# A new word table for batches 2 to 5: the products with w of tiles 3 and 4 beside the next batch's products with v, tile 5 beside its second scores

## The chip, the cores and the metric

The kernel runs on one core of a Trainium2 chip. The metric is device time in microseconds (us), the median of several runs.

## The reference

Eight batches of attention in two stages, and a layer with a maximum of three products behind it. `sm_attn` is softmax attention with a row maximum; heads have 64 columns.

```python
p_packed = sm_attn(p, k, v)                 # 32 packed queries, 576 keys, 8 heads, 8 batches
out = sm_attn(q, p_packed, p_packed)        # 576 queries on the 32 packed rows
x = out.transpose(0, 2, 1, 3).reshape(B * S, H * D)          # 4608 x 512
h = maximum(maximum(x @ w1, x @ w2), x @ w3)                 # 4608 x 768
return h @ w_out                                             # 4608 x 512
```

## The kernel before

Per batch the work falls into stages, each a Python generator that issues some instructions and yields. A **word** of a table advances one generator by one step: a letter, the batch (0 this one, 1 the next) and what else it needs, and at its end `v`, `g` or `a` for VectorE (DVE), GpSimd (POOL) or ScalarE (ACT) where the engine can be chosen. `P03` is a step of this batch's `project` of tile 3, `V101` one of the next batch's `values`. The order of words is the order of instructions on every engine and DMA queue; `START` holds the words of batches 0 and 1 and `LOOP` those of one batch, run for b = 2 to 7. There is no other scheduler.

The stages that matter here, with their lines:

- `S` scores (L253), products of the packed queries with k; `A` weigh (L266 maximum, L271 exp); `X` spread (L315): DVE transposes the weights into `x`, which goes to DRAM as `xk` (L318) and comes back as `xt` in four transfers (L322).
- `V` values (L342): 80 products with v, 64 of form 128\*32 (rows by columns of the array) and then 16 of form 64\*32. `K` packed (L357): one transpose and a copy, `pt`.
- `Q` queries (L370): second scores, 32 products of form 64\*32. `B` attend: transposes into `e` (L393), maximum (L397), subtraction (L399, POOL unless told otherwise), exp, sum `z2` (L404), reciprocal, product (L413), transpose `et` (L416), and the operands `a2h` (L131 or L133) and `a2l` (L136).
- `P` project (L442): w is multiplied by the packed rows, 16 products of form 64\*32 for a tile; ACT makes `ph` (L453) and DVE `pl` (L455). Two halves (r = 0 and 1) of a tile go to two PSUM tiles of the pool `ps_moe` (four buffers) for tiles 0 and 3, to one of `ps_big` (two buffers) for the others.
- `N` layer_in (L477): the large products. Six tiles of 128 hidden columns, each six steps (half `hf`, matrix `i`) of six products of 128\*128 into one `ps_moe` buffer `mi{b}_{tile}_{hf}_{i}`. `E` maximum: a copy out of the first buffer (L131 on ACT, L133 on DVE) and two maxima (L491, DVE), into `r{b}_{pair of tiles}`.
- `H` halves (L515 differences, then `yah`, `yal`, ... by L131/L133 and L136); `O` layer_out (L546), 14 groups of 9 products; `F` finish, with the stores.

A "burst" below is a run of small products (forms other than 128\*128) between large ones. A product in `N` waits until the step that had its `ps_moe` buffer four buffers earlier has been copied or taken into a maximum.

Of the kernel before, what the change touches and what calls it, by code (L numbers as in the profile page):

```python
# [20 lines left out]
B, H, S, D, NP = 8, 8, 576, 64, 32  # L21
# [52 lines left out]


LOOP = """
S1 A10 N02 N02 N02 N02 A11 N02 E020v A10 E020 E020 N00 N00 E021v E000 Z10 X1 E021 N02 A11 P03 X1 P05 E021 H02v
P03 P04 N01 N00 v11 N00 v10 P03 P03 P03 E001 q10 N03 N03 N00 N00 H02g E000 N03 N03 N03 E030v E030 E010 N01 Z11
N03 E000 E001 E001 H00v H00 H02v E031v P04 q11 E030 H00 N01 E031 E031 P04 E010 E010 N01 N01 N01 E011 E011 E011
X1 V101 V101 H03g H03 N04 N04 N04 N04 P05 k20 K1 E041 N04 H03v N04 H01g H01v H01v K1 Q1 E040v H01 H01 H03 H03  # L80
P05 E040 E041 E040 E041 B11 B11 N05 N05 N05 N05 B10 E050 E050 H04 B10 E050 N05 B11 H04 H04 E051 E051 N05 E051
P10 B11 B10 P11 P12 H05 H05 B11 H05v P10 O0 O0 P10 O0 B10 B10 B11v H05v P12 P11 F0 B10v P10 O0 F0 H01v H03v
H05 O0 O0 F0 H05 B11 F0 P12 B10 k21 B10g O0 O0 O0 F0 P11 F0 F0 O0 B10 F0 B11g B11 F0 F0 B10g B10v P10 B11g F0
F0 O0 O0 O0 F0 F0 B11v O0 F0 F0
"""


# [1 line left out]
def fused_kernel(ctx: ExitStack, tc: tile.TileContext, kp, qt, va, vb, wi, wo, out):  # L89
# [48 lines left out]
    def doze(n):  # L138

        for i in range(0, n, 4):  # L140
            k = min(n - i, 4)
            ps = ps_moe.tile([P, 512], F32, name=f"idle{len(dozes)}", tag="moe")
            dozes.append(ps)
            nc.tensor.matmul(  # L144
                out=ps[:, 0:k * P], lhsT=ident, rhs=ident.unsqueeze(1).to_broadcast([P, k, P]),
                start=True, stop=True,
            )
# [280 lines left out]
    def project(b, j):  # L428

        parts = [slice(0, R)]  # L430
        if j == 0 and b != 1 or j == 3 and b >= 2:

            parts = [slice(r, r + 1) for r in range(R)]
            ps = [ps_moe.tile([P, 512], F32, name=f"pw{b}_{j}_{r}", tag="moe") for r in range(R)]
            src = [x[:, 0:NW * P].unsqueeze(1) for x in ps]
        else:
            x = ps_big.tile([P, R, 512], F32, name=f"pw{b}_{j}", tag="big")
            ps, src = [x[:, r] for r in range(R)], [x[:, :, 0:NW * P]]
        for n in range(4):
            for r in range(R):  # L440
                o = slice(64 * r, 64 * r + 64)
                nc.tensor.matmul(  # L442
                    out=ps[r][NP * n:NP * n + NP, 0:NW * P],
                    lhsT=pt_sb[b % 2][o, NP * n:NP * n + NP],
                    rhs=w_sb[o, j, n * NW * P:(n + 1) * NW * P],
                    start=True, stop=True,
                )
        yield 1
        hi = pool.tile([P, R, NW * P], F32R, name=f"ph{b}_{j}", tag="ph", bufs=3)
        lo = pool.tile([P, R, NW * P], F32R, name=f"pl{b}_{j}", tag="pl", bufs=3)  # L450
        pw[b, j] = (hi, lo)
        for r, x in zip(parts, src):
            nc.scalar.activation(out=hi[:, r], in_=x, func=AF.Copy, scale=2.0 ** -WS)  # L453
            yield 1
            nc.vector.scalar_tensor_tensor(  # L455
                out=lo[:, r], in0=x, scalar=2.0 ** -WS, in1=hi[:, r].bitcast(F32), op0=ALU.mult, op1=ALU.subtract,
            )
            yield 1
# [148 lines left out]
    def weigh_and_turn(b, r):  # L607
# [5 lines left out]
    stages = {  # L613
        "S": scores, "A": weigh_and_turn, "Z": invert, "X": spread, "V": lambda b, *rs: values(b, rs), "K": packed, "Q": queries,
        "B": attend, "C": convert, "P": project, "N": layer_in, "E": maximum, "H": halves,
        "O": layer_out, "F": finish, "W": weights,
    }
# [3 lines left out]
    def run(words, base):  # L621

        for word in words.split():
            name = word.rstrip("vga")
            chosen[0] = word[len(name):] or None
            kind, x = name[0], [int(i) for i in name[1:]]
            if kind == "J":
                doze(int(name[1:]))
                continue
            if kind not in "wCW":  # L630
                x[0] += base
                if x[0] >= B:
                    continue
            if kind in loads:
                loads[kind](*x)
            else:
                key = (kind, *x)
                if key not in begun:
                    begun[key] = stages[kind](*x)
                next(begun[key], None)  # L640
        chosen[0] = None

    with tc.manual_schedule():
        run(START, 0)
        for b in range(2, B):
            run(LOOP, b)


# [41 lines left out]
```

## Time and profile before

| | us |
|---|---|
| median of 3 runs | 468.36 (468.21 to 468.43) |
| the profiled execution | 468.03 |
| its span, first to last instruction | 466.2 |

The profiled execution is 1.8 us longer than its span, and 0.33 us under the median. S of batches 3 to 7 begins at 142.92, 197.16, 251.37, 305.62 and 359.82 us, and the end of the last of these periods is 413.98.

### The profile page before, as it was taken

Reading aid. Unit: us, or ns where it says so; the run is one execution under the profiler, and the core shown is the slowest. Engines: PE = TensorE matmul, PEld = TensorE weight load, DVE = VectorE, ACT = ScalarE, POOL = GpSimd, SP = SyncE. Lnnn points to the kernel's source line nnn. Section 1 sums busy time; section 2 is a strip of 40 time slices with the busy share of each in tenths; the row PEclk is TensorE's granted clock in tenths of the full one; section 3 lists DMA queues with packets and bytes.
Section 4 is the critical chain, followed back from the end, with each engine's and each line's share of the span. In section 5 each row is a group of like instructions: output and inputs, shape, how many; then the busy total and the mean of one; then the engine's idle time right before and its main releaser. Section 6 shows DMA issues by size and latency. Waiting matters only on the chain.

```text
span 466.2 us, 11503 instructions
## 1 busy us (share of the span) xinstructions
PE 457.3 (98%) x4728; PEld 405.3 (87%) x4728; DVE 349.8 (75%) x763; ACT 172.6 (37%) x333; POOL 207.1 (44%) x180
## 2 busy tenths in 40 slices
PE   8899999999999999999999999999999999999996
PEld 3456987998998998989899898989989898998996
DVE  1799989999887677766888678786777678865652
ACT  3486975744332236022340226122350324402330
POOL 0357766756332156503653055612565036531542
PEclk9999999999999999999999999999999999999999
DMA  8999883011127510193104820075101820020002
GB/s 301 403 381 312 315 296 130 1 58 56 57 73 247 192 58 1 49 308 108 59 27 141 257 100 1 27 250 188 59 1 62 296 52 1 27 76 1 2 4 99
DMA packets 25540, 59.20 MB, mean 127 GB/s; under 512 B 2448, under 2 KB 15760, under 8 KB 25488
## 3 DMA queue, kind: packets, MB, share of 16 engines
q1 hardware_dynamic: 25488, 58.47, 36.7%
q8 instruction: 37, 0.61, 0.5%
q14 instruction: 15, 0.12, 0.1%
HBM read 45.48 MB, written 12.98 MB: 125 GB/s over the span
## 4 chain that ended last, share of the span: by engine, by line
PE 92%; DVE 4%; DMA 2%; ACT 0%; issue 0%; POOL 0%; POOLq 0%; ACTq 0%
PE mi L477 49%; PE mo L546 29%; PE pw L442 7%; DMA kt<-in_kp 2%; PE s L253 2%; PE av L342 2%; PE s L370 1%; PE idle L144 1%; DVE mx L266 1%; DVE xt L219 0%; DVE w_sb L203 0%; DVE r L491 0%; ACT a L271 0%; PE tp L342 0%; DVE xl L136 0%
## 5 line engine op out<-in xcount | busy, mean ns | idle before, releaser
L477 PE MATMUL mi<-a2h,ph 128*128 128x288 f32 x576 | 173.9, 302 | 0.7 <-ACT r L131 0.5
L477 PE MATMUL mi<-a2l,ph 128*128 128x288 f32 x576 | 169.7, 295 | 0.0
L477 PE MATMUL mi<-a2h,pl 128*128 128x288 f32 x576 | 169.7, 295 | 0.0
L477 PEld LDWEIGHTS mi<-a2h,ph 128*128 128x128 f32 x576 | 108.1, 188 | 15.5 <-issue 7.1
L477 PEld LDWEIGHTS mi<-a2h,pl 128*128 128x128 f32 x576 | 108.1, 188 | 0.0
L477 PEld LDWEIGHTS mi<-a2l,ph 128*128 128x128 f32 x576 | 108.1, 188 | 0.0
L491 DVE TENSOR_TENSOR r<-mi,r 128x288 f32<-128x288 f32 x192 | 83.3, 449 | 32.6 <-PE mi L477 30.2
L131 ACT COPY r<-mi 128x288 f32<-128x288 f32 x60 | 23.4, 401 | 122.8 <-PE mi L477 122.7
L455 DVE SCALAR_TENSOR_TENSOR pl<-pw,ph 128x768 fp32r<-128x768 f32 (+1 forms) x61 | 46.8, 775 | 4.5 <-ACT ph L453 3.6
L453 ACT ACTIVATE ph<-pw 128x768 fp32r<-128x768 f32 (+1 forms) x61 | 39.9, 675 | 18.8 <-PE pw L442 15.1
L546 PE MATMUL mo<-ych,xl 128*128 128x288 f32 x144 | 42.5, 295 | 0.0
L546 PE MATMUL mo<-ych,xh 128*128 128x288 f32 x144 | 42.4, 295 | 0.0
L546 PE MATMUL mo<-ycl,xh 128*128 128x288 f32 x144 | 42.4, 294 | 0.0
L136 POOL TENSOR_TENSOR yal<-r,yah 128x576 fp32r<-128x576 f32 x13 | 18.6, 1430 | 46.1 <-ACT yah L131 46.1
L271 ACT ACTIVATE a<-s,nm 128x576 f32<-128x576 f32 x16 | 11.9, 741 | 66.8 <-DVE nm L267 60.1
L442 PE MATMUL pw<-w_sb,pt 64*32 64x384 f32 x768 | 36.0, 487 | 0.3 <-POOL w_sb L207 0.3
L207 POOL TENSOR_TENSOR w_sb<-w_sb,wi 128x512 int32<-128x512 int32 x18 | 24.2, 1349 | 26.7 <-DVE z L282 11.8
L515 POOL TENSOR_TENSOR r<-r 128x288 f32<-128x288 f32 (+1 forms) x25 | 27.9, 1128 | 17.5 <-issue 9.0
L133 POOL CAST yah<-r 128x576 fp32r<-128x576 f32 x6 | 4.0, 662 | 57.0 <-DVE r L515 57.0
L546 PE MATMUL mo<-yah,xh 128*128 128x288 f32 x96 | 28.8, 300 | 0.0
L133 DVE COPY r<-mi 128x288 f32<-128x288 f32 x36 | 16.3, 455 | 16.2 <-PE mi L477 16.2
L546 PE MATMUL mo<-ybh,xl 128*128 128x288 f32 x96 | 28.3, 295 | 0.0
(117 smaller groups left out, 885.2 us busy)
## 6 DMA issues: line engine op xcount, KB each, us to landing
kt<-in_kp SPq DMA_DIRECT2D x16, 640.0 KB, 5.2
wi<-in_wi SPq DMA_DIRECT2D x18, 512.0 KB, 6.9
v<-in_va SPq DMA_DIRECT2D x16, 512.0 KB, 5.9
q<-in_qt SPq DMA_DIRECT2D x14, 576.0 KB, 7.1
xk<-x SPq DMA_DIRECT2D x6, 576.0 KB, 4.9
wi<-in_wo SPq DMA_DIRECT2D x6, 512.0 KB, 5.0
out_t<-r SPq DMA_DIRECT2D x8, 288.0 KB, 2.2
out_t<-t SPq DMA_DIRECT2D x8, 288.0 KB, 2.3
```

The lines of the kernel that those rows point to most:

```text
L131: e.copy(out=out, in_=src)
L133: e.tensor_copy(out=out, in_=src)
L136: on(default).tensor_tensor(out=lo, in0=src, in1=hi.bitcast(F32), op=ALU.subtract)
L207: nc.gpsimd.tensor_tensor(out=dst.bitcast(I32), in0=dst.bitcast(I32), in1=up, op=ALU.add)
L271: nc.scalar.activation(out=a.rearrange("p (a b) -> p a b", a=2), in_=s[:, :, 0:HS], func=AF.Exp, bias=nm, scale=SCALE, accum_out=z,)
L442: nc.tensor.matmul(out=ps[r][NP * n:NP * n + NP, 0:NW * P], lhsT=pt_sb[b % 2][o, NP * n:NP * n + NP], rhs=w_sb[o, j, n * NW * P:(n + 1) * ...
L453: nc.scalar.activation(out=hi[:, r], in_=x, func=AF.Copy, scale=2.0 ** -WS)
L455: nc.vector.scalar_tensor_tensor(out=lo[:, r], in0=x, scalar=2.0 ** -WS, in1=hi[:, r].bitcast(F32), op0=ALU.mult, op1=ALU.subtract,)
L477: nc.tensor.matmul(out=sums[b, j, hf, x][:, 0:HS], lhsT=w[:, r, x * P:(x + 1) * P], rhs=a[:, c], start=(r == 0 and n == 0), stop=(r == R - ...
L491: nc.vector.tensor_tensor(out=h, in0=sums[b, j, hf, i][:, 0:HS], in1=h, op=ALU.max)
L515: less = lambda out, x, y: on("g").tensor_tensor(out=out, in0=x, in1=y, op=ALU.subtract)
L546: nc.tensor.matmul(out=ps[:, 0:HS], lhsT=w[:, x, m * P:(m + 1) * P], rhs=h[:, z], start=(p == 0 and i == 0), stop=(p == NQ - 1 and i == 2),)
```

## The change

The old `LOOP` becomes `LAST` and is run for b = 6 and 7; a new `LOOP` is run for b = 2 to 5. In the new one the steps of tiles 0, 1 and 2 are interleaved, tiles 3 and 4 of `project` stand straight before V, tile 5 behind Q, the next batch's three tiles (10, 12, 11) inside the steps of tile 5, and many copies, maxima, differences and attend steps stand elsewhere or on another engine. Tile 5 of `project` uses two `ps_moe` tiles in these batches.

```diff
 LOOP = """
+S1 N02 v11 A10 N00 E020a N01 A10 N01 N00 N02 A11 N01 N00 v10 E010 N00 N02 E010 E000 N00 A11 N01 N02 X1 X1 E020
+N01 N02 N02 E001 N00 E021a E000 E000 X1 E010 P03 Z11 Z10 E020 E001 E011 E011 P03 E021 P04 V101 N01 P03 E001 P04
...
+LAST = """
...
-        if j == 0 and b != 1 or j == 3 and b >= 2:
+        if j == 0 and b != 1 or j == 3 and b >= 2 or j == 5 and 2 <= b < B - 2:
...
-            run(LOOP, b)
+            run(LOOP if b < B - 2 else LAST, b)
```

The changed file's lines are 12 higher. In the rows below the first number of a name is the batch, `pw4_3_0` the half 0 of tile 3 of batch 4.

TensorE before the change, the end of the burst of products with w of batch 4 (the two halves of tile 3 alternate in the six rows ahead; the products with v of batch 5 follow 96 large products later):

```order
L442 MATMUL pw4_3_0_3662<-w_sb_74,pt0_75 32x384
L442 MATMUL pw4_3_1_3663<-w_sb_74,pt0_75 32x384
L442 MATMUL pw4_5_3676<-w_sb_74,pt0_75 32x384 x8
L442 MATMUL pw4_4_3690<-w_sb_74,pt0_75 32x384 x8
L477 MATMUL mi4_1_0_0_3699<-a2h4_0_3500,ph4_1_3389 128x288
```

TensorE after it, the same place in the same burst:

```order
L454 MATMUL pw4_3_0_3749<-w_sb_74,pt0_75 32x384
L454 MATMUL pw4_3_1_3750<-w_sb_74,pt0_75 32x384
L454 MATMUL pw4_4_3773<-w_sb_74,pt0_75 32x384 x8
L354 MATMUL av5_3782<-v10_3654,xt5_3743 32x64 x2
L354 MATMUL av5_3782<-v11_3589,xt5_3743 32x64 x2
```

Tiles 3 and 4 now run straight into the products with v; tile 5 has gone to the second scores.

GpSimd before, around the difference `r4_2` of tile 4 (L515):

```order
L515 TENSOR_TENSOR r4_1_3619<-r4_1_3619 128x2x288
L515 TENSOR_TENSOR r4_2_3946<-r4_2_3946 128x288
L399 TENSOR_TENSOR e5_1_3999<-e5_1_3999,m2_5_1_0_4002 128x576
L136 TENSOR_TENSOR yal4_2_4051<-r4_2_3946,yah4_2_4049 128x576
```

GpSimd after it, around the same subtraction `e5_1`:

```order
L411 TENSOR_TENSOR e5_0_3944<-e5_0_3944,m2_5_0_0_3963 128x576
L527 TENSOR_TENSOR r4_0_3657<-r4_0_3657 128x288
L411 TENSOR_TENSOR e5_1_3993<-e5_1_3993,m2_5_1_0_3996 128x576
L148 TENSOR_TENSOR ybl4_1_4058<-r4_1_3603,ybh4_1_3974 128x576
L527 TENSOR_TENSOR r4_0_3657<-r4_0_3657 128x2x288
```

The difference `r4_2` has left GpSimd, and `ybl4_1` now stands behind `e5_1`. VectorE before the change, around the maxima of tile 4:

```order
L133 COPY r4_2_3946<-mi4_4_0_0_3912 128x288
L455 SCALAR_TENSOR_TENSOR pl4_5_3941<-pw4_5_3676,ph4_5_3940 128x768
L491 TENSOR_TENSOR r4_2_3946<-mi4_4_0_1_3919,r4_2_3946 128x288
L491 TENSOR_TENSOR r4_2_3946<-mi4_4_1_1_3948,r4_2_3946 128x288
L491 TENSOR_TENSOR r4_2_3946<-mi4_4_0_2_3926,r4_2_3946 128x288
L491 TENSOR_TENSOR r4_2_3946<-mi4_4_1_2_3956,r4_2_3946 128x288
L393 STREAM_TRANSPOSE e5_1_3999<-s2_5_0_3969 128x288
L393 STREAM_TRANSPOSE e5_1_3999<-s2_5_1_3978 128x288
L397 TENSOR_REDUCE m2_5_1_0_4002<-e5_1_3999 128x18
```

VectorE after it, from the last maximum of the first half of tile 4 (ahead of it stand the maximum of `mi4_4_0_1`, two of tile 3 and one `pl`):

```order
L503 TENSOR_TENSOR r4_2_3922<-mi4_4_0_2_3956,r4_2_3922 128x288
L148 TENSOR_TENSOR yal4_0_3984<-r4_0_3657,yah4_0_3891 128x576
L405 STREAM_TRANSPOSE e5_1_3993<-s2_5_0_3873 128x288
L405 STREAM_TRANSPOSE e5_1_3993<-s2_5_1_3882 128x288
L409 TENSOR_REDUCE m2_5_1_0_3996<-e5_1_3993 128x18
L145 COPY r4_2_3922<-mi4_4_1_0_3976 128x288
L503 TENSOR_TENSOR r4_2_3922<-mi4_4_1_1_4000,r4_2_3922 128x288
L503 TENSOR_TENSOR r4_2_3922<-mi4_4_1_2_4011,r4_2_3922 128x288
L527 TENSOR_TENSOR r4_2_3922<-r4_2_3922 128x288
L416 TENSOR_REDUCE z2_5_0_0_4060<-e5_0_3944 128x18
L416 TENSOR_REDUCE z2_5_1_0_4062<-e5_1_3993 128x18
L503 TENSOR_TENSOR r4_2_3922<-mi4_5_0_1_4064,r4_2_3922 128x288
```

VectorE has got the difference (L527), between the maxima of tile 4 and two sums of 576 columns; and the copy of `mi4_4_1_0`, which ScalarE made before, behind the transposes and the reduction of `e5_1`.

## Rows read from the trace of the kernel before

**Rows 1.** The page: the span, the busy time of each engine with its share.

```profile
span 466.2 us, 11503 instructions
PE 457.3 (98%) x4728; PEld 405.3 (87%) x4728; DVE 349.8 (75%) x763; ACT 172.6 (37%) x333; POOL 207.1 (44%) x180
```

**Rows 2.** Busy time by stretch, the period of one batch from S to S: length, busy time of PE, PEld, DVE, ACT and POOL, granted clock of TensorE (share of full speed), DMA share and GB/s.

```profile
251.37:305.62 54.25, 54.25 (x585) 49.37 (x584) 40.72 (x92) 16.14 (x32) 22.54 (x19) 1.00 0.35 113
```

**Rows 3.** Timeline of PE around the burst of the products with w (start, duration, engine, line, operation, form, count).

```profile
204.61 0.29 PE L477 MATMUL mi<-a2l,ph 128*128 128x288 f32 x1
204.83 2.17 PE L442 MATMUL pw<-w_sb,pt 64*32 64x384 f32 x48
206.93 0.40 PE L477 MATMUL mi<-a2h,ph 128*128 128x288 f32 x1
207.17 0.29 PE L477 MATMUL mi<-a2h,pl 128*128 128x288 f32 x1
```

**Rows 4.** The weight loads of the same burst (PEld): eight loads to a group.

```profile
205.18 0.15 PEld L442 LDWEIGHTS pw<-w_sb,pt 64*32 64x32 f32 x8 [0.17 <-issue]
205.50 0.15 PEld L442 LDWEIGHTS pw<-w_sb,pt 64*32 64x32 f32 x8 [0.17 <-issue]
```

**Rows 5.** Busy time by stretch of the products with v alone (L342; length, PE, PEld, granted clock, DMA): the change from form 128\*32 to 64\*32, and the last 16 products.

```profile
220.74:220.88 0.15, 0.15 (x16) 0.06 (x5) 1.00 0.00 0
220.88:221.25 0.36, 0.36 (x23) 0.27 (x16) 1.00 0.00 0
```

**Rows 6.** Timeline of PE where, in `START`, the products with v of batch 2 are followed at once by 16 with w.

```profile
68.76 1.38 PE L342 MATMUL av<-v,xt 128*32 128x64 f32 x73
69.93 0.51 PE L442 MATMUL pw<-w_sb,pt 64*32 64x384 f32 x1
70.04 0.82 PE L442 MATMUL pw<-w_sb,pt 64*32 64x384 f32 x12
70.79 0.40 PE L477 MATMUL mi<-a2h,ph 128*128 128x288 f32 x1
```

**Rows 7.** Timeline where a buffer is copied out by ACT while only one other step runs, in the order of their starts.

```profile
263.50 0.29 PE L477 MATMUL mi<-a2l,ph 128*128 128x288 f32 x1
263.84 0.70 ACT L131 COPY r<-mi 128x288 f32<-128x288 f32 x2 [2.89 <-PE mi L477]
264.30 0.19 PEld L477 LDWEIGHTS mi<-a2h,ph 128*128 128x128 f32 x1
```

**Rows 8.** Timeline where PE waited for DVE, in `START`.

```profile
94.61 0.81 DVE L491 TENSOR_TENSOR r<-mi,r 128x288 f32<-128x288 f32 x2
95.11 0.19 PEld L477 LDWEIGHTS mi<-a2h,ph 128*128 128x128 f32 x1 [0.48 <-DVE r L491]
95.22 0.19 PEld L477 LDWEIGHTS mi<-a2h,pl 128*128 128x128 f32 x1
```

**Rows 9.** Timeline of DVE: maxima, a difference, transposes and reductions, and what starts behind each.

```profile
267.02 0.46 DVE L491 TENSOR_TENSOR r<-mi,r 128x288 f32<-128x288 f32 x1 [0.17 <-PE mi L477]
267.51 0.46 DVE L515 TENSOR_TENSOR r<-r 128x288 f32<-128x288 f32 x1
...
276.37 0.75 DVE L136 TENSOR_TENSOR ybl<-r,ybh 128x576 fp32r<-128x576 f32 x1
277.04 0.45 DVE L515 TENSOR_TENSOR r<-r 128x288 f32<-128x288 f32 x1
277.41 0.45 DVE L133 COPY r<-mi 128x288 f32<-128x288 f32 x1
...
282.38 0.75 DVE L397 TENSOR_REDUCE m<-e 128x18 f32<-128x576 f32 x1
283.05 0.84 DVE L393 STREAM_TRANSPOSE e<-s 128x288 f32<-128x288 f32 x2
283.81 0.42 DVE L491 TENSOR_TENSOR r<-mi,r 128x288 f32<-128x288 f32 x1
```

**Rows 10.** Timeline of DVE and of POOL at the end of a period, and of POOL earlier in it.

```profile
302.02 0.55 DVE L455 SCALAR_TENSOR_TENSOR pl<-pw,ph 128x384 fp32r<-128x384 f32 x1
302.49 0.45 DVE L565 SCALAR_TENSOR_TENSOR s<-mo,v 128x288 f32<-128x288 f32 x1
303.73 1.79 DVE L136 TENSOR_TENSOR a2l<-et,a2h 128x576 fp32r<-128x576 f32 x1
303.48 1.42 POOL L594 TENSOR_TENSOR t<-v,t 128x576 f32<-128x576 f32 x1
283.21 1.16 POOL L399 TENSOR_TENSOR e<-e,m 128x576 f32<-128x576 f32 x1 [1.22 <-DVE m L397]
284.33 1.42 POOL L136 TENSOR_TENSOR yal<-r,yah 128x576 fp32r<-128x576 f32 x1
```

**Rows 11.** Timeline of SP's queue for batch 5, the summary of the tile `xt`, and PE's timeline at V of this batch.

```profile
259.73 0.33 SPq L318 DMA_DIRECT2D xk<-x  x1
263.80 1.75 SPq L322 DMA_DIRECT2D xt<-xk  x4
DMA to landing us min/median/max: 2.7/3.2/4.9
274.09 1.46 PE L342 MATMUL av<-v,xt 128*32 128x64 f32 x80
```

More of the change, by code (lines that the diff above doesn't have):

```diff
@@ L76 @@
 LOOP = """
+S1 N02 v11 A10 N00 E020a N01 A10 N01 N00 N02 A11 N01 N00 v10 E010 N00 N02 E010 E000 N00 A11 N01 N02 X1 X1 E020
+N01 N02 N02 E001 N00 E021a E000 E000 X1 E010 P03 Z11 Z10 E020 E001 E011 E011 P03 E021 P04 V101 N01 P03 E001 P04
+P03 E021 q11 V101 K1 P03 H02g q10 N03 K1 P04 E030a H00g E011 N03 N03 Q1 H00g H01v P05 E030 H01g N04 N03 E040a
+P05 N03 k20 E030 N04 B10 N03 H02v N04 B10 E031a P05 E040 P05 E031 H02g E031 P05 H03a N04 E040 H00v N05 B11 B11
+B10 B10 N04 H01g E041v B11 E041 N04 E041 P10 P12 E050 H04v P11 B11 P11 H04 P10 H03 B10 B11 N05 H01 N05 E050 H03g
+H04 E050 N05 B10a N05 E051v P12 E051 P10 N05 O0 E051 H03 B11a O0 H01 H01v O0 H03v H05 H05v F0 F0 O0 O0 F0 H05v
+H05v H03v B10 F0 H05 O0 H05v O0 B11 O0 O0 F0 P12 F0 B10g F0 O0 B11v O0 F0 F0 B11 F0 B10 O0 F0 k21 F0 O0 P10 B10a
+B11a B10g P11 F0 F0 O0 F0 P10 F0 B11g
+"""
+LAST = """
 S1 A10 N02 N02 N02 N02 A11 N02 E020v A10 E020 E020 N00 N00 E021v E000 Z10 X1 E021 N02 A11 P03 X1 P05 E021 H02v
@@ L81 @@
 P05 E040 E041 E040 E041 B11 B11 N05 N05 N05 N05 B10 E050 E050 H04 B10 E050 N05 B11 H04 H04 E051 E051 N05 E051
-P10 B11 B10 P11 P12 H05 H05 B11 H05v P10 O0 O0 P10 O0 B10 B10 B11v H05v P12 P11 F0 B10v P10 O0 F0 H01v H03v
-H05 O0 O0 F0 H05 B11 F0 P12 B10 k21 B10g O0 O0 O0 F0 P11 F0 F0 O0 B10 F0 B11g B11 F0 F0 B10g B10v P10 B11g F0
-F0 O0 O0 O0 F0 F0 B11v O0 F0 F0
+P10 B11 B10 P11 P12 H05 H05 B11 H05v P10 O0 O0 P10 O0 B10 B10 B11v H05v P12 P11 F0 B10v P10 O0 F0 H01v H03v H05
+O0 O0 F0 H05 B11 F0 P12 B10 k21 B10g O0 O0 O0 F0 P11 F0 F0 O0 B10 F0 B11g B11 F0 F0 B10g B10v P10 B11g F0 F0 O0
+O0 O0 F0 F0 B11v O0 F0 F0
 """
```

## The prediction, made before the changed kernel ran

> **What bounds the kernel now.** I read the page first, then busy time by period, then the timeline of TensorE at every burst, then DVE and POOL where they work together. TensorE is busy 457.3 of 466.2 us [rows 1], and in a period of batches 3 to 7 for 54.25 of 54.25 at the full granted clock [rows 2]: between 142.92 and 413.98 it waits for nobody. So nothing is gained by having data earlier there; the change gains only by what the products themselves cost in another order, and loses by every wait it brings. DVE is busy 40.72 of 54.25, POOL 22.54 [rows 2]: neither is full, but each can be late at one place. The numbers of products, copies and maxima stay the same; all terms below are for one batch, and there are four such batches.
>
> **What a burst costs, and what is saved.** Large products follow at .13 us (a step of six: .80). In [rows 3] the burst with w starts .22 behind the last large product, .09 more than the pitch. Its six groups of eight are .325 apart [rows 4], so 6 x .325 = 1.95, but it lasts from 204.83 to 206.93, 2.10: .15 more, of which I put .02 on its first group and .13 on its end, where the next large product starts later than a seventh group would. That product is followed at .24 instead of .13, another .11. A whole burst thus has .09 + .02 at its entry and .24 at its exit.
>
> The new order puts tiles 3 and 4 straight before V. That takes away the exit of one burst (.24) and the entry of the other (.11), .35 in all, and puts the passage from form 64\*32 to 128\*32 in their place. The other bursts are as many as before: tile 5 stands behind Q instead of between tiles 3 and 4, with forms alike, and the next batch's three tiles are still one burst between large products, so I cost both at nothing in TensorE's own time. The passage is not in the trace. Its nearest row is the opposite one inside V: from 220.74 to 220.88, .15 us, the loads were busy for only .06 [rows 5]; 64 products end there and 16 of the other form begin. The other bound is [rows 6]: there 16 products with w started (69.93) among the 64\*32 products of V's end, as if nothing had to empty, but both have one form. I take .16, so the gain is .35 - .16 = **.195**; with nothing to empty it is .35, with .25 for the passage .10.
>
> By the Trainium skill, "TensorEngine Tiling (Array Packing)", Key Properties, a change of tiling mode, and not just of tile, empties the engine. That speaks for .16 here and against the .35 of a free passage; by it the four batches gain .78 and not 1.4. The row at 220.74 agrees, with its .15.
>
> **Where single-step waits appear.** With tiles 0, 1 and 2 (and 3, 4) interleaved, some steps reuse a buffer of `ps_moe` whose step ended only one step before, so a copy or maximum has six products' time. The order has one such place per batch for ACT before, five for DVE after. For ACT: the products end at 263.79, the copy is one .35 piece of 263.84 to 264.54 and PE's load starts 264.30 without a wait [rows 7]. For DVE: the first maximum of 94.61 releases the load at 95.11, .50 later, and PE's next load follows .11 behind [rows 8]. Six products (.80) leave some .47 for that, less the .16 by which a product outlasts the pitch, the .04 to DVE's start and the .13 by which a load goes ahead; so each costs about .02 when DVE is free: 4 to 5 of them, **.08** (bounds 0, if PE's queue hides it, and .25, if DVE is behind by a short instruction).
>
> **The wait at the next batch's first products.** Call 0 the time at which TensorE could start them. The second of them needs the buffer of the copy of `mi4_4_1_0`, which stands on DVE behind the transposes and reduction of `e5_1`. DVE can begin the chain with the maximum of `mi4_4_0_1`, whose products end six steps and one entry back (4.89), plus .20 for the last product to end: -4.69. From there, by the distances in [rows 9, 10]: to the next maximum .37, to the one that needs its result .49, to `pl` .37, to the maximum behind it .47, to `yal` .37, to the transposes .67, to the reduction .76 and .10, to the copy .67: it starts at -.42, ends at +.04, and PE knows .055 later. TensorE stands still for about **.1** (0 to .3).
>
> **DVE and GpSimd in each other's way.** This is the large term. Behind that copy DVE makes two maxima and the difference `r4_2`, each on the result ahead of it: -.40 + 3 x .49 = 1.08. POOL meanwhile makes `e5_1`: the reduction ends at -.30, POOL starts .08 later, and its next instruction, `ybl4_1`, 1.12 after that [rows 10]: +.90, and runs 1.43, to 2.33. In [rows 10] a DVE difference of two SBUF tiles that starts at 303.73, .25 after a POOL addition (303.48 + 1.42 = 304.90), takes 1.79 instead of the .75 of its like at 276.37 [rows 9], and ends .62 after POOL's end. All five batches show this pair. The difference `r4_2` starts .18 behind `ybl4_1`, has half the columns, and so ends some .32 after 2.33, at 2.65 instead of 1.54: 1.1 late. Late next are two sums (.67 each) and the maximum of `mi4_5_0_1` behind them: it starts at 3.91, ends at 4.37, and TensorE knows at 4.42. The step that needs its buffer comes two steps after the burst: 2.10 + .90 + .80 = 3.80, with the wait above 3.9. Its first product goes .1 after the release, at about 4.5. The cost is **.6**; before, a difference of that pair stood on POOL, and the sums behind more maxima. Bounds: 0 if the two are not simultaneous (their starts differ by .18 only), and .8 if later maxima are caught as well.
>
> The Trainium skill, "SBUF — State Buffer", Who interferes with whom, has this as an exclusive lock: a DVE instruction with two SBUF inputs and a GpSimd instruction that reads SBUF exclude each other, and the first to start keeps the other out. By that rule alone `r4_2` waits for the whole of `ybl4_1`, as above; the 1.79 us row agrees, less the .13 by which it ended early.
>
> **Transfers.** V moves forward, to about 16.3 after S. `x` is ready at about 6.9 (two maxima, two exps and four transposes behind S, estimated from their durations). From the issue of `xk` to the first of `xt` 4.07, to the last issue 1.3 more, and 2.7 to 4.9 to landing [rows 11]: `xt` lands 15.0 to 17.2 after S. Before, it had landed by about 270 of V's 274.09. Mostly hidden; where the longest landing occurs TensorE waits up to .9. I add nothing to the centre and keep it for the range.
>
> **The sum.** Per batch -.195 + .08 + .1 + .6 = +.58, times four +2.3 us on the profiled 468.03: 470.3. The profile lies .33 under the median of the runs shown, so **470.6 us**.
>
> **The rivals.**
> - *Nothing is caught.* If POOL's `ybl4_1` starts after the difference instead of .18 ahead of it (then POOL waits, and nobody needs `ybl4_1` for some 6 us), the .6 falls away: -.195 + .18 = about 0 a batch, 468.3; without the two small waits -.78, 467.6. For it: the two starts are close, each an accumulation of eight estimated distances. Against: both hang on the same reduction on DVE, so they move together.
> - *Faster: the passage is free.* If the 64\*32 products run into V without emptying, .35 a batch, and neither wait occurs: -1.4, 466.95. It is faster as soon as the waits stay under .1 a batch. For it: [rows 6]. Against: the two forms differ here, and there they didn't.
> - *`xt` comes late as well.* V waits .3 to .9 in two or more of the four batches, on top of the forecast: 471.2 to 472.5. For it: the margin falls from about 4 us to between +1.3 and -.9. Against: the median landing of 3.2 leaves .8.
> - *The change does nothing.* The new burst is there in the order, so the .35 that goes is certain; only the sum with the waits can be nil, which the first rival holds.
>
> **How the numbers follow.** About .2% (.94 us) is what a measurement of this kernel can tell from no change. The forecast with its own range 469.5 to 471.2 has .45, the late `xt` .12, nothing caught .30, the free passage .13. The first two are slower: .57; the third is within .2%: .30; the last is faster: .13. The range runs from the free passage's edge, 467.3, to 472.0 in the late `xt`.
>
> **What would show it.** In the trace after: no burst between tiles 3, 4 and V, and .15 to .17 from the last start of the products with w to the first with v; the period longer by .4 to .8 with PE idle in one place, behind DVE's maximum of tile 5's first half, some 35 us after S; DVE's difference of tile 4 there lasting 1.5 us or so with a POOL instruction of 1.43 ending under it. Wrong is the forecast if PE's waits in a period sum to under .2, or if the difference lasts .46.

## The result, and the profile after

| | before | after |
|---|---|---|
| median, us | 468.24 (467.89 to 468.43) | 470.72 (470.39 to 471.14) |
| span of the profiled execution | 466.2 | 468.9 |

The changed kernel takes 1.0057 times as long, with a 95% interval of 1.0046 to 1.0067: 2.2 to 3.1 us slower. Forecast was 470.6.

The page of the changed kernel, span and busy time by engine, against [rows 1]:

```profile
span 468.9 us, 11494 instructions
PE 458.0 (98%) x4728; PEld 407.5 (87%) x4728; DVE 345.9 (74%) x747; ACT 180.2 (38%) x361; POOL 205.5 (44%) x176
```

TensorE has the same 4728 products, .7 us more of busy time, and 2.7 us more of span. Busy time by period (length, busy time of PE, PEld, DVE, ACT and POOL, granted clock, DMA share, GB/s), one of the four changed periods:

```profile
197.80:252.69 54.89, 54.53 (x584) 49.96 (x584) 39.75 (x87) 18.06 (x39) 22.15 (x19) 1.00 0.35 111
```

The four periods are 54.92, 54.89, 54.91 and 54.90. Before, the same four were 54.24, 54.21, 54.25 ([rows 2] shows this one) and 54.20, in the mean 54.23. So each is longer by .66 to .70, .68 in the mean: 2.7 in all, the whole difference of the spans. For the first time TensorE is idle in them, .36 to .37 in each. The waits of PE between 142.88 and 362.50 (engine and line, what it waited for, us in total, times, longest) are one group, once in each period:

```profile
PE mi L489 <- DVE r L503: 1.5, 4, 0.4
```

Its place, on PE's timeline from the next batch's products with w into tile 5:

```profile
228.89 2.31 PE L454 MATMUL pw<-w_sb,pt 64*32 64x384 f32 x48
231.13 0.40 PE L489 MATMUL mi<-a2h,ph 128*128 128x288 f32 x1
...
232.69 0.29 PE L489 MATMUL mi<-a2l,ph 128*128 128x288 f32 x1
233.34 0.40 PE L489 MATMUL mi<-a2h,ph 128*128 128x288 f32 x1 [0.36 <-DVE r L503]
233.57 0.29 PE L489 MATMUL mi<-a2h,pl 128*128 128x288 f32 x1
```

Two losses stand here. The burst of 48 products lasts 228.89 to 231.13, 2.24, where the like of it took 2.10 [rows 3]: .14. Two steps behind it, the next product comes .65 after the last one instead of .13: .52, of which the profile shows .36 as idle, since a product's modelled end lies behind the pitch. The product behind it follows at .23 (233.34 to 233.57) where diff_psum, a run without this wait, has .16: another .07, so some .6 in all. What DVE and POOL did meanwhile:

```profile
228.54 0.45 DVE L145 COPY r<-mi 128x288 f32<-128x288 f32 x1
229.09 1.02 DVE L503 TENSOR_TENSOR r<-mi,r 128x288 f32<-128x288 f32 x2
230.14 1.45 DVE L527 TENSOR_TENSOR r<-r 128x288 f32<-128x288 f32 x1
231.52 1.40 DVE L416 TENSOR_REDUCE z<-e 128x18 f32<-128x576 f32 x2
232.84 1.01 DVE L503 TENSOR_TENSOR r<-mi,r 128x288 f32<-128x288 f32 x2
...
228.75 1.16 POOL L411 TENSOR_TENSOR e<-e,m 128x576 f32<-128x576 f32 x1 [0.79 <-PE mi L489]
229.87 1.41 POOL L148 TENSOR_TENSOR ybl<-r,ybh 128x576 fp32r<-128x576 f32 x1
```

Read it downwards: the copy begins .35 before the burst and ends .10 into it; the difference (L527) begins .27 behind `ybl` and lasts 1.45 where others of its form take .46 [rows 9]; two sums follow; the maximum for which TensorE waits begins at 232.84, 3.95 after the burst's start. The gain stands earlier in the period, on PE's timeline:

```profile
212.64 1.52 PE L454 MATMUL pw<-w_sb,pt 64*32 64x384 f32 x32
214.09 1.46 PE L354 MATMUL av<-v,xt 128*32 128x64 f32 x80
215.48 0.40 PE L489 MATMUL mi<-a2h,ph 128*128 128x288 f32 x1
```

The products with w of tiles 3 and 4 take 1.45 to the first with v, those with v 1.39 as before, and no large product stands between.

### The profile page after: what moved, and what is told of

It reads as the page before. It is cut to its first block, busy times and chain, and to the rows that moved or that the text cites. A ratio compares the mean times of both kernels' runs of the same rounds, so it can differ in the third digit from the quotient of the medians.

```text
span 468.9 us, 11494 instructions
## 1 busy us (share of the span) xinstructions
PE 458.0 (98%) x4728; PEld 407.5 (87%) x4728; DVE 345.9 (74%) x747; ACT 180.2 (38%) x361; POOL 205.5 (44%) x176
## 4 chain that ended last, share of the span: by engine, by line
PE 83%; DVE 11%; DMA 4%; issue 1%; SPq 1%; ACT 0%; POOL 0%; DVEq 0%
PE mi L489 44%; PE mo L558 29%; PE pw L454 5%; DVE r L503 3%; DMA kt<-in_kp 2%; PE av L354 2%; PE s L265 2%; DMA q<-in_qt 1%; PE s L382 1%; DVE z L416 1%; DVE r L527 1%; DVE e L405 1%; DVE m L409 1%; DVE mx L278 1%; DVE yal L148 1%
## 5 line engine op out<-in xcount | busy, mean ns | idle before, releaser
L527 POOL TENSOR_TENSOR r<-r 128x288 f32<-128x288 f32 (+1 forms) x37 | 38.2, 1045 | 84.7 <-DVE r L503 49.4
L143 ACT COPY r<-mi 128x288 f32<-128x288 f32 x72 | 27.8, 400 | 118.6 <-PE mi L489 118.5
L467 DVE SCALAR_TENSOR_TENSOR pl<-pw,ph 128x384 fp32r<-128x384 f32 (+1 forms) x65 | 47.4, 738 | 17.4 <-ACT ph L465 17.1
L465 ACT ACTIVATE ph<-pw 128x384 fp32r<-128x384 f32 (+1 forms) x65 | 41.0, 644 | 41.6 <-PE pw L454 26.6
L454 PE MATMUL pw<-w_sb,pt 64*32 64x384 f32 x768 | 37.4, 487 | 0.3 <-POOL w_sb L219 0.3
L558 PE MATMUL mo<-ybh,xh 128*128 128x288 f32 x96 | 28.3, 295 | 0.0
L558 PE MATMUL mo<-yal,xh 128*128 128x288 f32 x96 | 28.3, 295 | 0.0
L558 PE MATMUL mo<-ybl,xh 128*128 128x288 f32 x96 | 28.3, 295 | 0.0
L558 PE MATMUL mo<-yah,xl 128*128 128x288 f32 x96 | 28.3, 295 | 0.0
```

The lines of the kernel that those rows point to most:

```text
L143: e.copy(out=out, in_=src)
L454: nc.tensor.matmul(out=ps[r][NP * n:NP * n + NP, 0:NW * P], lhsT=pt_sb[b % 2][o, NP * n:NP * n + NP], rhs=w_sb[o, j, n * NW * P:(n + 1) * ...
L467: nc.vector.scalar_tensor_tensor(out=lo[:, r], in0=x, scalar=2.0 ** -WS, in1=hi[:, r].bitcast(F32), op0=ALU.mult, op1=ALU.subtract,)
L527: less = lambda out, x, y: on("g").tensor_tensor(out=out, in0=x, in1=y, op=ALU.subtract)
L558: nc.tensor.matmul(out=ps[:, 0:HS], lhsT=w[:, x, m * P:(m + 1) * P], rhs=h[:, z], start=(p == 0 and i == 0), stop=(p == NQ - 1 and i == 2),)
```

## The experiments

The theory: the merged burst saves one entry and one exit, less one passage between forms; the loss is a DVE difference of two SBUF tiles that GpSimd's `ybl` keeps out, with a late copy in front of it. Its rivals: the maximum is late because of DVE's order alone; the small products pass freely. All times below are against runs of the kernel before on the same chip; periods are the mean of those of the changed batches, from the start of one batch's first scores to the next; the kernel before has 54.23.

| run | us | before | ratio | 95% interval | period |
|---|---|---|---|---|---|
| after | 470.72 | 468.24 | 1.0057 | 1.0046 to 1.0067 | 54.91 |
| ybl_early | 468.52 | 468.15 | 1.0010 | 1.0001 to 1.0019 | 54.31 |
| diff_psum | 468.37 | 468.15 | 1.0006 | .9998 to 1.0015 | 54.31 |
| copy_act | 467.98 | 468.15 | .9995 | .9987 to 1.0004 | 54.16 |
| v_first | 476.24 | 468.15 | 1.0178 | 1.0160 to 1.0196 | 56.1 to 57.4 |
| p4_alone | 473.27 | 468.05 | 1.0112 | 1.0097 to 1.0126 | 55.46 |
| tail_first | 470.51 | 468.05 | 1.0052 | 1.0039 to 1.0065 | 54.79 |
| best | 467.37 | 468.05 | .9986 | .9977 to .9995 | 54.02 |
| best_b6 | 469.07 | 468.05 | 1.0023 | 1.0014 to 1.0032 | 54.09 |
| best_slot | 467.02 | 468.12 | .9976 | .9967 to .9985 | 53.93 |
| best_again | 467.07 | 468.12 | .9981 | .9972 to .9990 | 54.02 |

### ybl_early: GpSimd's subtraction goes first

```diff
-B10 B10 N04 H01g E041v B11 E041 N04 E041 P10 P12 E050 H04v P11 B11 P11 H04 P10 H03 B10 ...
+B10 B10 N04 H01g H03 E041v B11 E041 N04 E041 P10 P12 E050 H04v P11 B11 P11 H04 P10 B10 ...
```

> POOL's 128x576 subtraction `ybl` of tile pair 1 goes ahead of the subtraction `e5_1` in batches 2 to 5; DVE's and TensorE's order stay. Theory 'exclusion' (a DVE difference of two SBUF tiles and a POOL instruction keep each other out, so that the difference of tile 4 lasts 1.45 us instead of .46): `ybl` is now over when the difference starts, at most the end of `e5_1` overlaps it; the difference lasts .46 to .8, TensorE's .5 wait in tile 5 falls to under .15, and a period takes 54.3 to 54.5 instead of 54.91: 468.3 to 469.2 us. Rival 'DVE's queue' (the maximum of tile 5 is late because two sums and the difference stand ahead of it, whatever POOL does): DVE's order is unchanged, so the wait stays at .5 and the time at 470.7.

DVE's and POOL's timelines at the same place:

```profile
229.87 0.63 DVE L527 TENSOR_TENSOR r<-r 128x288 f32<-128x288 f32 x1
...
227.65 1.42 POOL L148 TENSOR_TENSOR ybl<-r,ybh 128x576 fp32r<-128x576 f32 x1
229.03 1.16 POOL L411 TENSOR_TENSOR e<-e,m 128x576 f32<-128x576 f32 x1
```

The period, busy time by stretch:

```profile
197.52:251.82 54.30, 54.30 (x584) 49.96 (x583) 39.00 (x87) 18.07 (x39) 22.18 (x19) 1.00 0.35 112
```

With DVE's order untouched and `ybl` ahead of it, the difference lasts .63 (it still meets the end of `e5_1`, 230.19), PE has no wait in the page's sense, and the period falls by .60. The rival "DVE's queue" alone falls. What is left above the kernel before is small: 1.0001 to 1.0019.

### diff_psum: one input from PSUM

```diff
-            less(r[:, 1], r[:, 1], r[:, 0])
+            if j == 4 and 2 <= b < B - 2:
+                less(r[:, 1], sums[b, 4, 1, 2][:, 0:HS], r[:, 0])
+            else:
+                less(r[:, 1], r[:, 1], r[:, 0])
```

> Only the first input of the difference of tile 4 is changed, in batches 2 to 5: it is read from the PSUM buffer of the last product step (`mi` half 1, matrix 2) instead of the SBUF tile, so the values differ from the reference's; places, shapes and order of all instructions stay, POOL's `ybl` runs beside it as now. 'Exclusion' through the two SBUF inputs: the difference lasts about .46 us, ends 1 us earlier, TensorE's wait in tile 5 goes, a period takes 54.3 to 54.4 us: 468.2 to 468.8. 'DVE's queue': the difference still ends late or the wait stays above .3; 470 or more.

DVE's and POOL's timelines:

```profile
229.52 0.46 DVE L527 TENSOR_TENSOR r<-mi,r 128x288 f32<-128x288 f32 x1
...
229.25 1.42 POOL L148 TENSOR_TENSOR ybl<-r,ybh 128x576 fp32r<-128x576 f32 x1
```

This is the clean test: it computes other values, but at the same place and in the same order the difference begins .27 behind `ybl` as in the changed kernel, and lasts .46 in the middle of it. Only one of the two SBUF inputs was taken away, and the period fell by .60 as in the run before. So it is the pair of SBUF inputs and not the time, the shape or the neighbour as such.

### copy_act: the late copy

```diff
-B10 B10 N04 H01g E041v B11 ...
+B10 B10 N04 H01g E041a B11 ...
```

> The copy out of the first buffer of tile 4's second half, for which the second product of the next batch's first tile waits, is made by ScalarE instead of DVE (batches 2 to 5). My step of the prediction (DVE reaches this copy .1 late): the burst of 48 products with w falls from 2.24 to 2.10 us. DVE's next maxima start earlier as well, so the difference of tile 4 starts ahead of `ybl`, beside `e5_1` on POOL, and ends about .9 earlier: the wait in tile 5 goes too, a period takes 54.2 to 54.4 us, 467.9 to 468.8. If the burst is long for another reason (its tiles' order), it stays at 2.24.

PE's timeline at the burst, then DVE's and POOL's:

```profile
228.01 2.17 PE L454 MATMUL pw<-w_sb,pt 64*32 64x384 f32 x48
230.11 0.40 PE L489 MATMUL mi<-a2h,ph 128*128 128x288 f32 x1
...
228.70 0.65 DVE L527 TENSOR_TENSOR r<-r 128x288 f32<-128x288 f32 x1
...
227.88 1.16 POOL L411 TENSOR_TENSOR e<-e,m 128x576 f32<-128x576 f32 x1 [0.79 <-PE mi L489]
229.00 1.64 POOL L148 TENSOR_TENSOR ybl<-r,ybh 128x576 fp32r<-128x576 f32 x1
```

The burst is back at 2.10 (228.01 to 230.11): the .14 was this copy. The difference now comes before `ybl`; it waits for the end of `e5_1`, and then `ybl` is the one that is kept out, 1.64 instead of 1.41, which nobody notices. One letter in the table takes away both losses: 54.16, .07 less than before the change. In the time (.9987 to 1.0004) this can't be told from the kernel before.

### v_first: the other order inside the burst

```diff
-... X1 E010 P03 Z11 Z10 E020 E001 E011 E011 P03 E021 P04 V101 N01 ...
+... X1 E010 V101 P03 Z11 Z10 E020 E001 E011 E011 P03 E021 P04 N01 ...
```

> In batches 2 to 5 the products with v go ahead of those with w of tiles 3 and 4 instead of behind them, in the same burst. Theory 'the passage from form 64*32 to 128*32 empties the array': the burst begins from large products as every burst, V's last 16 products have the form of those with w, and the passage costs nothing: the two bursts together fall from 2.84 us (1.45 + 1.39) to 2.67 to 2.72, a period by .12 to .17 to about 54.76: 470.0 to 470.3 us. Rival 'all small products pass freely, and the .14 at the end of the products with w belongs to them': 2.84 as now, 470.7. Rival 'transfers': V now comes 1.45 us earlier than `xt`'s latest landing allows; TensorE waits before V in some batches, up to 1 us, 471 to 473.

PE's timeline:

```profile
216.40 1.38 PE L354 MATMUL av<-v,xt 128*32 128x64 f32 x73 [1.62 <-DMA xt<-xk]
217.57 0.51 PE L454 MATMUL pw<-w_sb,pt 64*32 64x384 f32 x1
...
217.68 1.47 PE L454 MATMUL pw<-w_sb,pt 64*32 64x384 f32 x28
219.76 0.40 PE L489 MATMUL mi<-a2h,ph 128*128 128x288 f32 x1 [0.61 <-DVE pl L467]
```

The rival "transfers" came in, dearer than it said (476.24 against 471 to 473): TensorE waits for `xt` in all four batches, up to 1.6. A second wait stood in no expectation: the products with w now end 1.4 later, and tile 3's `pl` is late for its first step. Beside these waits the passage is as the theory has it: products with w start among V's last ones. After a burst with w the next large product starts .07 before the modelled end of the burst (230.18 and 230.11 in copy_act); by that, without its wait it would have started at 219.08, an estimate, 2.68 after 216.40, where the changed kernel took 2.84 (212.64 to 215.48). The time of this run can't test the passage; tail_first does.

### p4_alone: one burst more

```diff
-N01 N02 N02 E001 N00 E021a E000 E000 X1 E010 P03 ... E021 P04 V101 N01 ...
+N01 N02 N02 E001 P04 N00 E021a E000 E000 X1 E010 P03 ... E021 V101 N01 ...
```

> Part of the change undone: in batches 2 to 5 the 16 products with w of tile 4 stand one step (six large products) ahead of the burst again, as a burst of their own. Prediction's price of a whole burst (.09 + .02 at its entry, .24 at its exit, .35 in all): a period goes from 54.91 to 55.26, the time to 472.1. Rival 'a burst costs only the waits that it brings': 54.91 and 470.7.

PE's timeline:

```profile
267.60 0.88 PE L454 MATMUL pw<-w_sb,pt 64*32 64x384 f32 x16
268.40 0.40 PE L489 MATMUL mi<-a2h,ph 128*128 128x288 f32 x1
...
269.39 0.88 PE L454 MATMUL pw<-w_sb,pt 64*32 64x384 f32 x16
270.20 1.46 PE L354 MATMUL av<-v,xt 128*32 128x64 f32 x80
...
272.61 0.33 PE L369 MATMUL av<-ident,pp 128*128 128x128 f32 x1
272.70 0.38 PE L489 MATMUL mi<-a2h,ph 128*128 128x288 f32 x1
```

From the start of tile 4's products to V: 2.60, of which six large products at the pitch are .80 and the 32 products with w in one burst 1.45: .35, the price forecast. The period grew by .55, though. The other .2 is at the transpose K: the large product behind it starts 2.50 after V (270.20 to 272.70) instead of 2.31 (214.09 to 216.40, below), and K itself 2.41 instead of 2.29. The burst ahead of V is now shorter by tile 4, so when V ends (271.59) DVE is still at the two maxima behind tile 3's `pl`, and `pp`, which K needs, stands behind them. DVE's timeline, and PE's weight load for K:

```profile
270.88 0.56 DVE L467 SCALAR_TENSOR_TENSOR pl<-pw,ph 128x384 fp32r<-128x384 f32 x1 [3.52 <-ACT ph L465]
271.36 0.81 DVE L503 TENSOR_TENSOR r<-mi,r 128x288 f32<-128x288 f32 x2
272.09 0.47 DVE L364 TENSOR_SCALAR pp<-av,r 128x64 f32<-128x64 f32 x2
...
272.61 0.14 PEld L369 LDWEIGHTS av<-ident,pp 128*128 128x128 f32 x1 [0.19 <-DVE pp L364]
```

The changed kernel's K, on PE's timeline:

```profile
216.38 0.27 PE L369 MATMUL av<-ident,pp 128*128 128x128 f32 x1
216.40 0.38 PE L489 MATMUL mi<-a2h,ph 128*128 128x288 f32 x1
```

### tail_first: like forms beside each other

```diff
-        for t, r in [(t, r) for ts in (range(SF), (SF,)) for r in rs for t in ts]:
+        for t, r in [(t, r) for ts in ((SF,), range(SF))[::1 if 3 <= b < B - 1 else -1] for r in rs for t in ts]:
             n = P if t < SF else SR
+            first, last = (SF, SF - 1) if 3 <= b < B - 1 else (0, SF)
...
-                    start=(t == 0), stop=(t == SF),
+                    start=(t == first), stop=(t == last),
```

> In batches 3 to 6 the products with v run their 16 of form 64*32 first and the 64 of form 128*32 behind them, at the place that the change gave them; so the products with w (64*32) run into the like form, and the only passage is that inside V, in the other direction. Theory 'each passage between forms costs about .15': the two bursts fall from 2.84 to 2.67 to 2.70 us, a period from 54.91 to 54.76, the time to 470.1. Rival 'the end of the products with w costs .14 whatever comes next': 2.84, 470.7. Rival 'the passage towards more rows is dearer than that towards fewer': 2.75 to 2.84.

PE's timeline:

```profile
267.78 1.52 PE L455 MATMUL pw<-w_sb,pt 64*32 64x384 f32 x32
269.10 1.45 PE L355 MATMUL av<-v,xt 64*32 64x64 f32 x80
270.48 0.40 PE L490 MATMUL mi<-a2h,ph 128*128 128x288 f32 x1
```

The products with w take 1.32 to the first with v instead of 1.45, and those with v 1.38 with their passage in the other direction. The same products in another order: 2.70 for 2.84, and .12 a period. The passage is real, and what it costs is .13 to .14.

### best, best_again and best_slot: a faster version

best (and, unchanged, best_again) has the edits of copy_act and tail_first. best_slot adds one more: the first half of the next batch's tile 0 is evacuated before tile 5 goes on.

```diff
-... E041 P10 P12 E050 H04v P11 B11 P11 H04 P10 H03 B10 B11 N05 H01 ... P12 E051 P10 N05 O0 ...
+... E041 P10 P12 E050 P10 H04v P11 B11 P11 H04 H03 B10 B11 P10 N05 H01 ... P12 E051 N05 O0 ...
```

> The copy of tile 4's second half on ScalarE (as in the run copy_act, 54.15 a period) and the products with v with their 64*32 part first (batches 3 to 6). If the two gains add: 54.15 - .15 = 54.00 a period, 467.4 us, a ratio to the kernel before of about .998. If what is gained at the burst is waited for elsewhere (the weights of the next batch arrive from DRAM .4 us ahead of the products with v at the least): 54.15, 468.0.

> The kernel of the run best once more, beside the other of this call: 54.02 a period, a ratio to the kernel before of .9986 as measured, within its interval.

> As best, with the first half of the next batch's tile 0 taken out of its `ps_moe` buffer (`ph` on ScalarE, `pl` on DVE) ahead of the steps of tile 5 instead of between their last two, in batches 2 to 5. Theory 'the single-step waits come from the buffers that the next batch's first tile holds': the last steps of tile 5 and the first group of the output layer then reuse a buffer two steps old; the gaps there that are wider than the pitch (about .04 in tile 5, .07 at the first group) go, a period falls from 54.02 to 53.90 to 53.93: 466.9 to 467.1. Rival 'these gaps are TensorE's own at a change of operands': they stay, 54.02. If DVE is too late with `pl` for the third step: a wait of .1 to .5 there, 54.1 to 54.5.

A period of best, busy time by stretch:

```profile
197.13:251.13 54.00, 54.00 (x584) 49.55 (x583) 38.59 (x86) 18.35 (x40) 22.17 (x19) 1.00 0.35 113
```

And one of best_slot:

```profile
196.78:250.68 53.90, 53.90 (x584) 49.46 (x583) 38.64 (x86) 18.34 (x40) 22.20 (x19) 1.00 0.36 113
```

The gains add, twice measured (.9986 and .9981). PE's timeline at the first products of the output layer in best_again:

```profile
287.84 0.37 PE L559 MATMUL mo<-yah,xh 128*128 128x288 f32 x1
288.05 0.29 PE L559 MATMUL mo<-yah,xl 128*128 128x288 f32 x1
```

The same in best_slot:

```profile
287.82 0.30 PE L559 MATMUL mo<-yah,xh 128*128 128x288 f32 x1
287.96 0.30 PE L559 MATMUL mo<-yah,xl 128*128 128x288 f32 x1
```

The .21 between the two products becomes .14: a wait of .07 that no row names as one, since TensorE counts as busy. With the gaps of the same kind in tile 5 it is .1 a period, as expected. So most of the single-step waits come from the two buffers that the next batch's tile 0 held. best_slot is faster than both kernels: .9976, .9967 to .9985. Its gain over best_again shows in the periods alone (53.93 against 54.02, some .4 us in four); in the time, 467.02 against 467.07, it is not resolved.

### best_b6: one batch too many

```diff
-            run(LOOP if b < B - 2 else LAST, b)
+            run(LOOP if b < B - 1 else LAST, b)
...
-... N05 B10a N05 E051v P12 ...
+... N05 B10a N05 E051a P12 ...
```

> As best, with the new table run for batch 6 as well, the products with v 64*32 part first in batch 7 too, and the copy of tile 5's second half on ScalarE as well. Each change is worth what it was in the batches before: one more period at 54.0 instead of 54.2 (-.2), and .03 a period where that copy had TensorE wait with only one step between: five times .03. 467.0 to 467.3 us. If batch 6 with the new table leaves work for the last batch that was done earlier, the end is later and the time 467.5 or more.

A miss: 1.0023. Two waits of PE behind 359 us, where best_again has only the second:

```profile
PE mi L490 <- POOL a2l L148: 0.7, 1, 0.7
PE mi L490 <- ACT r L143: 0.5, 1, 0.5
```

The operands `a2l` of the last batch are made by DVE in best; with the new table in the batch before, GpSimd makes them, behind two additions, and TensorE waits: that is the second outcome that the expectation names. Against best (467.37) the run loses 1.7 us, of which this wait is .7 and four periods longer by .07 are .3; the rest was not taken apart. Nor did the copy on ScalarE pay in the earlier batches (54.09 against 54.02); why, no run settles.

## Why the prediction was right

**The direction and the sum.** Forecast +.58 a batch, measured +.68; 470.6 forecast, 470.72 measured. That the two times lie only .1 apart is in part luck: the sum was .4 us short over four batches, and the forecast started from 468.36, where the kernel before measured 468.24 beside the changed one.

**Exclusion, .6.** The step that decided the outcome: without it the times are 1.0010 and 1.0006 times those of the kernel before. The difference was to begin .18 behind `ybl` and began .27 behind it; to end .32 after it, and ended .31 after (231.59 and 231.28); the maximum was to begin 3.91 after the burst's start, and began at 3.95. The wait it makes is .52, and .07 more at the product behind it. Taking `ybl` away, or one SBUF input, gave back .60 of a period each. By the Trainium skill, "SBUF — State Buffer", Who interferes with whom, a DVE instruction with at most one SBUF input, outside its 2-port modes, does not contend with GpSimd. The trace of diff_psum agrees, with .46 under a 1.42 us `ybl`. The rival "nothing is caught" would have needed the two starts the other way round, which copy_act shows: then it costs POOL .23 and TensorE nothing.

**The gain, .195.** copy_act, which has neither large wait, is .07 a period shorter than the kernel before, and holds .13 of single-step waits (below): .20. The parts hold too: the price of a burst, .35 forecast, .35 in p4_alone; the passage, .16 forecast, .13 to .14 by tail_first and, by estimate, .16 by v_first. The rival "the passage is free" falls with tail_first. One sign was stated wrongly: the distance from the last start of the products with w to the first with v was to be .15 to .17. That figure was what the passage adds, not the distance, which holds a last group's pitch as well; a reader who had looked for .16 there would not have found it. What was to be read there is .41, against .28 where the next product has the same form (tail_first): what the passage adds is the difference, as in 1.45 against 1.32.

**The late copy, .1.** Measured .14 to .15, and copy_act takes it away. It mattered more than its size, since it also decides who is first in the exclusion.

**Single-step waits, .08.** Measured some .13. TensorE's starts show them: in each period of copy_act and best_again four large products stand wider apart than the pitch of .13 (in the period of best_again shown above .15 at 277.68, .16 at 285.57, .15 at 287.18 and .21 at 288.05), in the kernel before none over .14 but those behind bursts. The price of .02 was about right for three of them and too small for the last, .06 to .07. The place was in the main another: the prediction named the stretches where tiles are interleaved, and only the first of the four lies in one (tiles 3 and 4); the other three went in best_slot, when the next batch's tile 0 gave its buffers back. With what was measured the sum is -.20 + .13 + .15 + .60 = .68: this term and the copy are each .05 of the .10 by which the forecast was short.

**Transfers, nothing added.** Right: in the changed periods PE has no wait for a DMA. The margin is as thin as was said. SP's queue in the changed kernel, the four transfers of `xt` for the V at 214.09:

```profile
207.47 1.75 SPq L334 DMA_DIRECT2D xt<-xk  x4
```

The summary of its tile `xt`:

```profile
DMA to landing us min/median/max: 2.7/3.1/4.9
```

The last of the four, issued at 208.79, took 4.9 and landed .4 before V's 214.09; v_first, whose V needs it 1.4 earlier, paid up to 1.6. In this batch the rival "`xt` comes late as well" was half a step of large products away; in the other three `xt` landed .9 to 1.2 ahead.

## What to carry to other kernels

When an order on a full engine is changed to save its own switching, cost the switches from the timeline (here .35 for a burst, .14 for a passage between forms), and then look on the other engines for two instructions that cannot run together, in the order in which they will now start: a .46 us difference that became 1.45 us cost three times the gain. Such a loss is repaired by letting the one that nobody waits for come second, not by less work: one copy moved to a less busy engine turned 1.0057 into .9995. Put small products of one form beside each other, and give back buffers before the stretch in which every step needs one.

## What was not expected of the hardware

- The blocked difference ended .31 behind GpSimd's instruction each time, whatever was left of that one: 231.59 and 231.28 in the changed kernel, 230.50 and 230.19 in ybl_early, 229.35 and 229.04 in copy_act. The other side is harmless here: in copy_act `ybl` took 1.64 for 1.41 behind the difference.
- The waits of .02 to .07 us stand in no list of waits: in best TensorE counts as busy for 54.00 of 54.00, and best_slot still found .1 there. Only the distance between starts shows them.
- A passage between forms costs about the same in both directions: with V's parts exchanged, V took 1.38 for 1.39, and inside V the first product of the other form starts .15 behind the last of the one before either way, where products of one form follow at .014.
